# A new written-out order for a fused linear-attention and token-mixing kernel, with constant matmuls ahead of the work, some wider tiles and joint reciprocals

## The chip, the cores and the metric

The kernel runs on one core of one Trainium2 chip. The core has engines that each work through a queue of their own: TensorE (PE, with its weight loads PEld), VectorE (DVE), ScalarE (ACT), GpSimd (POOL) and SyncE (SP), which here only issues DMAs. Times are device microseconds (us) of one execution. The kernel before the change takes 124.98 us, the median of three runs (124.4 to 125.5). The profile is one execution, recorded by the hardware profiler.

## What is computed

Inputs are q, k and v, each of 8 batches x 8 heads x 576 positions x 64, and three weight matrices, all float32. The output is 8 x 576 x 512 in float32. Cut to what matters:

```python
theta = pi/2 * arange(S) / S                      # S = 576
phi(x) = concat([relu(x)*cos(theta), relu(x)*sin(theta)])   # 64 -> 128 features
kv  = phi(k)^T v ;  z = sum_s phi(k)              # per batch and head
x   = (phi(q) kv) / (phi(q) z + 1e-6)             # heads side by side: 576 x 512 per batch
W   = (x w_q)(x w_k)^T / sqrt(64)                 # 576 x 576 per batch
out = relu(W x) w_out
```

The kernel never forms W: it computes `(x w_k)^T x` first, a 64 x 512 matrix, and multiplies `x w_q` with that.

## The kernel before

**Units.** The eight heads of a batch are worked on as two half batches of four heads; half batch H (0 to 15) belongs to batch H // 2. A half batch's q, k or v arrives in two DMAs of 288 KB ("halves" a and b, two heads each). The raw tiles have four buffers per tensor (slot H % 4), nearly all later tiles two. PSUM is one tile of 8 banks, and each PE step names the bank, or the first of two, that it writes.

**Steps.** The whole program is a list of words, `ORDER`. A word is a step's letters, the index, `:bank` for PE, and `@A`, `@V` or `@G` for a step that runs on ACT, DVE or POOL. The loop at L436 to L449 walks through the words and issues each step's instructions, so that every engine's queue holds its steps in the order of the words; waits between engines follow from the tiles that the steps read and write. There is no planner at run time: an engine whose next step has to wait stands still, whatever lies behind it.

- LK, LQ, LV (L131): loads on SP. LW (L417): the weights; w_out is one DMA of 1,024 KB. ST (L414): a store of one 128 x 512 result tile, on SP as well, so a store that waits for its tile holds up every load behind it.
- TK, TV, TQ, TW, T2, TI, TZ: sine tables, identity, zeroed padding.
- RK, RQ (L203): relu of k and q into bf16. CV (L210): v into bf16. VS (L213, DVE): v times cosine and sine.
- KV (L229, PE): k'v of a half batch, 36 small matmuls of 64 x 64 weights with 130 columns, and KE (L250): its copy out of PSUM. QT (L241, PE): q transposed, 18 transposes of 64 x 128. QM (L254, DVE): transposed q times cosine and sine.
- N (L263, PE): numerator and denominator of a quarter batch g (two per half batch, H = g // 2), 20 matmuls. EP (L276): denominator plus epsilon. X (L283, DVE): a reciprocal (L288) and the division (L289).
- XT or XR (PE): x transposed, by 10 whole or 20 half tiles; XE: its copy.
- WK, WQ, KX, MX (PE) with their copies KW, QW, XK, XA, XB, ME: the token mixing of a batch; MX and ME come four to a batch. WO (L400, PE): four matmuls of 128 x 512 for one of 36 output tiles; OE (L408): its copy; CW: casts of the weights.

WO tiles of two batches need the ME steps of those batches, so the first WO can't come before about the first four half batches are through; from then on PE alternates between WO and the steps of later half batches.

Of the kernel before, what the change touches and what calls it, by code (L numbers as in the profile page):

```python
# [29 lines left out]
LK4b RQ5@G LV7b X6 KW0@V EP7@A LQ6b LQ7a KV2:4 LV7a KE2@A N5:4 N4:6 LQ6a LK7b LK7a LV6a CV5@G CW0@A  # L30
X7 RK5@G WQ0:0 KX0:1 LV6b LK6a XT3:2 EP5@A EP4@A X5 XK0@A XA0@A QW0@A X4 LK6b LW2 QT5:4 XT2:6 VS5
MX0:0 QM5 XE3@A CV4@G RQ4@V XE2@A LV9a KV5:2 MX1:6 WQ1:4 ME0@A QT4:0 VS4 KE5@A ME1@A RK4@G N11:2
RQ7@G WK1:5 QM4 QW1@A EP11@A KW1@A N10:6 KX1:5 XB0@A EP10@A LQ9b KV4:0 LV9b XK1@A XA1@A X10 KE4@A
X11 CV7@G LV8b XB1@A N8:0 EP8@A N9:6 LQ9a LK9b X8 MX6:4 XT5:2 RQ6@G RK7@G LK9a EP9@V ME6@A MX2:4 X9
XE5@A VS7 QT7:0 XT4:6 ME2@A MX7:4 KV7:2 LQ8a XE4@A LV8a QM7 WK2:6 MX3:0 LK8a ME7@A QT6:4 KE7@A LQ8b
MX5:2 LK8b CV6@G KW2@A RK6@G CW5@G LQ10b KX2:6 ME3@A LQ11b WQ2:7 VS6 ME5@A QM6 N15:2 KV6:0 LV11
CW2@G MX4:4 XK2@A CV9@G RQ9@G EP15@V XB2@G QW2@A CW3@A X15 CW4@V KE6@A RK9@G LQ10a LV13b N14:6 N12:0
N13:2 ME4@A EP14@V LQ11a RQ8@G EP12@A WO6:4 LK11a X14 WO0:5 LK11b EP13@A XT7:6 X12 WO2:0 OE6:0@A
LV10b LK10b X13 XT6:2 RK8@G XA2@A WO8:1 XE7@A MX8:6 OE0:1@A QT9:4 VS9 XE6@V OE2:2@A CV11@G LV10a
OE8:3@A LK10a LK13b QM9 LK12a WK3:0 ME8@A CV8@A KV9:2 KW3@V KE9@V MX11:6 WQ3:1 KX3:0 ME11@A N18:2  # L40
MX9:6 MX10:4 QW3@A XK3@A EP18@A VS8 LV13a WO1:0 ME10@A X18 ME9@A QT8:4 OE1:4@A N19:2 EP19@A QM8
KV8:6 KE8@V WO10:0 N17:6 LV12b EP17@A RQ10@A X19 XB3@G N16:4 WO12:1 WO9:2 EP16@V LV12a RQ11@G LQ13b
OE10:5@A LK13a X17 OE9:6@A WO3:0 X16 XR8:4 XR9:2 RK11@G OE3:7@A XE8@A XA3@A QT10:6 WO4:0 CV10@G
QT11:4 VS11 OE4:8@A XE9@V LQ13a QM10 KV11:2 RK10@G ST2 OE12:9@A WK4:0 KE11@A MX15:2 CV13@G QM11
LV15b LQ12a MX12:6 ST1 LQ12b WQ4:1 ME15@A LV14b ME12@A N23:4 VS10 N22:2 RK13@G KW4@A MX13:6 EP22@V
LK12b ME13@A WO7:0 KV10:6 EP23@V X22 KX4:2 LV14a ST10 QW4@A KE10@A OE7:10@A X23 XK4@A RQ13@G N21:6
N20:4 LQ15b EP21@A VS13 MX14:2 XA4@A RQ12@G WO11:0 CV12@A WO5:1 ME14@A LQ15a OE11:2@A ST7 LQ14b X21
EP20@V KV13:6 KE13@A QT13:2 X20 LQ14a XR10:4 MX16:6 WO14:0 ME16@A OE5:4@A XB4@G VS12 XT11:6 WO16:1
QM13 XE11@V RK12@G XE10@A N27:2 MX18:4 LV15a OE16:11@A ME18@A EP27@A QT12:6 WO15:1 ST11 RQ15@G
OE14:5@A KV12:4 ST3 WQ5:0 QM12 X27 KE12@A CV14@G MX17:4 N26:6 LK15a EP26@V CV15@G MX19:2 QW5@A  # L50
ME17@A X26 ST5 WK5:0 ME19@A N24:4 OE15:10@V N25:2 XR13:6 LK15b KW5@A EP24@A ST15 KX5:0 RK15@G EP25@V
WO19:1 XE13@A WO21:6 XK5@A X25 X24 RQ14@A WO17:0 OE21:4@A OE19:7@A QT15:4 ST16 QT14:6 XR12:2 VS15
XE12@A LK14a WO13:1 QM15 KV15:4 XA5@A ST14 VS14 WK6:2 KE15@A LK14b OE13:5@A WO20:3 N31:4 QM14
OE17:11@A OE20:10@V EP31@V XB5@A ST20 RK14@V MX22:0 KW6@A MX21:6 ME22@A KX6:2 WQ6:3 ME21@A X31
KV14:0 N30:6 ST9 QW6@A XK6@A XA6@G MX20:4 ME20@A MX23:2 ST21 KE14@V WO18:0 XB6@G N29:4 ME23@A ST12
ST0 ST13 EP30@V X30 OE18:10@V EP29@A MX26:2 ST4 N28:6 EP28@A WO23:1 WO24:0 ME26@A MX25:2 ST6 X29
OE23:2@A OE24:4@A XR15:4 X28 XR14:6 WO26:0 XE15@V ST24 OE26:5@A WO25:1 XE14@V ME25@A OE25:8@V WK7:0
ST23 MX27:2 MX24:6 ME24@V ST26 KW7@A WQ7:1 KX7:0 ST18 XK7@A ST25 QW7@A ME27@V XB7@G WO22:6 WO28:7
XA7@A MX31:0 OE22:2@V OE28:10@A MX28:2 WO27:6 ST8 ME31@A MX30:0 ST19 ST28 OE27:3@A MX29:4 ME30@V
# [6 lines left out]
def kernel(  # L66
# [162 lines left out]
    def KV(H, ps, eng):  # L229
        place["KV", H] = ps  # L230
        kv_v = kv_view(ps)
        for c in range(C):
            for pr, r in ((0, 0), (1, 1), (1, 0), (0, 1)):
                a = slice(H2 * r, H2 * r + H2)
                o = slice(H2 * pr, H2 * pr + H2)
                nc.tensor.matmul(  # L236
                    kv_v[o, r, :], rk_b[H % NPREP][a, pr, c, :],
                    v2_b[H % NV2][a, pr, c, :, 0:D + 1],
                    start=(c == 0), stop=(c == C - 1))

    def QT(H, ps, eng):  # L241
        place["QT", H] = ps
        qt_v = qt_view(ps)
        for c in range(C):
            for r in range(2):
                a = slice(H2 * r, H2 * r + H2)
                nc.tensor.transpose(qt_v[:, r, c * H2:(c + 1) * H2],  # L247
                                    rq_b[H % NPREP][a, c, :, :], ident[a, a])
# [4 lines left out]

    def QM(H, ps, eng):  # L254
        V.tensor_mul(  # L255
            qm_b[H % NQM][:, :, :, 0:C, :].rearrange("p s r c d -> p s r (c d)"),
            qt_view(place["QT", H]).unsqueeze(1).to_broadcast([P, 2, 2, S]),
            qtab.rearrange("p s c d -> p s (c d)").unsqueeze(2).to_broadcast([P, 2, 2, S]))
# [4 lines left out]
    def N(g, ps, eng):  # L263
        H, r = divmod(g, 2)
        place["N", g] = ps
        nv = num(ps)
        for u in range(SC):
            for s in range(2):
                for pr in range(2):
                    a = slice(H2 * pr, H2 * pr + H2)  # L270
                    nc.tensor.matmul(  # L271
                        nv[:, pr, u, :], qm_b[H % NQM][a, s, r, 2 * u:2 * u + 2, :],
                        kv_b[H % 2][a, r, s, 0:D + 1],
                        start=(u == 0 and s == 0), stop=(u == SC - 1 and s == 1))

    def EP(g, ps, eng):  # L276
        den = num(place["N", g])[:, :, :, D:D + 1]
        if eng is A:
            A.activation(rec_b[g % 8], den, AF.Identity, bias=eps_t)  # L279
        else:  # L280
            V.tensor_scalar(rec_b[g % 8], den, EPS, None, op0=ALU.add)

    def X(g, ps, eng):  # L283
# [4 lines left out]
        V.reciprocal(rec, rec)  # L288
        V.tensor_tensor(  # L289
            x_b[b % NX][:, :, 4 * h:4 * h + 4, :].rearrange(  # L290
                "p u (w r) d -> p r w u d", r=2)[:, r],
            nv[:, :, :, 0:D], rec.to_broadcast([P, 2, SC, D]), op=ALU.mult)
# [187 lines left out]
```

## Time and profile before

| | |
|---|---|
| median of three runs | 124.98 us |
| span of the profiled execution, first to last instruction | 122.35 us |
| DMA traffic of the kernel | 39.07 MB |
| last matmul ends | 118.64 us into the span |

The span is 2.63 us shorter than the median; the time of a run also has what lies outside the first and last instruction. In the pages of the profile each line is a group of instructions with its busy time, and the chain of waits is followed back from the last instruction. The clock row is the TensorE clock that the profiler recorded. Matmuls are pipelined, so that the mean duration of one matmul is longer than the time by which it moves the queue; the latter is read from the chain, which gives whole runs of matmuls by their length.

### The profile page before, as it was taken

How to read it: one execution, taken by the hardware profiler on the slowest of the kernel's cores; microseconds unless marked ns; L12 is line 12 of the kernel's file. 1: busy time of each engine (PE TensorE's matmuls, PEld its weight loads, DVE VectorE, ACT ScalarE, POOL GpSimd, SP SyncE). 2: the span in 40 equal slices, each digit the busy share in tenths (PEclk: the TensorE clock that was granted, in tenths of full speed). 3: DMA queues.
4: the chain of work that ended last, by engine and by line, in shares of the span. 5: the costliest groups of instructions: out<-in, count | busy, mean ns of one | idle time of the engine just before them, and what ended most of it. 6: DMA issues, size and time to landing. Idle time of an engine off the chain costs nothing.

```text
span 122.3 us, 5248 instructions
## 1 busy us (share of the span) xinstructions
PE 97.3 (80%) x2250; PEld 65.4 (53%) x2266; DVE 92.0 (75%) x136; ACT 80.8 (66%) x151; POOL 55.2 (45%) x63
## 2 busy tenths in 40 slices
PE   0015878859987796989997959899999999999970
PEld 0013766758776574656572636556765665563420
DVE  0226999896998996997989695996899998764420
ACT  7245858612888886587935837889787986557260
POOL 7764030747369999777492386548120020010000
PEclk9999999999999999999999999999999999999997
DMA  3999999999999999999999996399249069596975
GB/s 115 311 379 404 397 389 388 385 404 384 393 391 384 399 401 397 391 390 396 390 393 392 408 392 259 117 331 296 105 152 303 1 250 358 188 351 259 359 267 211
DMA packets 20614, 39.39 MB, mean 322 GB/s; under 512 B 3184, under 2 KB 3184, under 8 KB 20592
## 3 DMA queue, kind: packets, MB, share of 16 engines
q1 hardware_dynamic: 20592, 39.07, 87.1%
q8 instruction: 17, 0.28, 0.9%
q14 instruction: 5, 0.04, 0.1%
HBM read 29.62 MB, written 9.44 MB: 319 GB/s over the span
## 4 chain that ended last, share of the span: by engine, by line
PE 61%; DMA 18%; issue 7%; DVE 5%; ACT 5%; SPq 1%; DVEq 0%; ACTq 0%
PE ps L405 24%; PE ps L271 8%; PE ps L236 6%; DMA qraw<-in_q_dram 5%; PE ps L335 5%; DMA vraw<-in_v_dram 5%; DMA kraw<-in_k_dram 4%; PE ps L362 4%; PE ps L247 3%; PE ps L348 3%; DMA out_dram<-o 3%; PE ps L302 3%; PE ps L385 3%; DVE x L289 3%; PE ps L315 2%
## 5 line engine op out<-in xcount | busy, mean ns | idle before, releaser
L405 PE MATMUL ps<-wow,mix 128*128 128x512 bf16 x128 | 33.5, 381 | 2.0 <-issue 1.0
L215 DVE TENSOR_TENSOR v<-vb,vtab 128x2304 bf16<-128x2304 bf16 (+1 forms) x17 | 23.4, 1374 | 6.2 <-POOL vb L197 6.2
L289 DVE TENSOR_TENSOR x<-ps,rec 128x640 bf16<-128x640 f32 x32 | 26.4, 825 | 1.9
L255 DVE TENSOR_TENSOR qm<-ps,qtab 128x2304 bf16<-128x2304 bf16 x16 | 21.5, 1351 | 3.1 <-PE ps L247 3.1
L195 ACT COPY o<-ps 128x512 f32<-128x512 f32 x29 | 16.5, 587 | 9.2 <-PE ps L405 7.7
L191 POOL TENSOR_SCALAR rk<-kraw 128x1152 bf16<-128x1152 f32 (+1 forms) x13 | 17.2, 1320 | 8.6 <-ACT mix L396 2.8
L236 PE MATMUL ps<-v,rk 64*64 64x130 bf16 x576 | 13.4, 243 | 9.5 <-ACT rk L189 8.9
L405 PEld LDWEIGHTS <-mix 128*128 128x128 bf16 x144 | 12.5, 98 | 15.6 <-issue 2.9
L271 PE MATMUL ps<-kvs,qm 64*128 64x65 bf16 x640 | 16.2, 203 | 4.7 <-ACT kvs L195 1.7
L396 ACT ACTIVATE mix<-ps 128x576 bf16<-128x576 f32 x28 | 17.7, 654 | 3.2 <-PE ps L385 2.6
L197 POOL TENSOR_SCALAR vb<-vraw 128x1152 bf16<-128x1152 f32 (+1 forms) x14 | 15.1, 1082 | 9.9 <-DMA vraw<-in_v_dram 6.7
L191 POOL TENSOR_SCALAR rq<-qraw 128x1152 bf16<-128x1152 f32 (+1 forms) x11 | 14.2, 1296 | 11.4 <-DMA qraw<-in_q_dram 5.1
L271 PEld LDWEIGHTS <-qm 64*128 64x128 bf16 x640 | 13.8, 102 | 8.4 <-issue 5.3
L236 PEld LDWEIGHTS <-rk 64*64 64x64 bf16 x576 | 10.7, 120 | 12.4 <-ACT rk L189 9.1
L195 ACT COPY xT<-ps 128x1280 bf16<-128x1280 bf16 (+1 forms) x11 | 12.9, 1178 | 2.2 <-PE ps L302 1.1
L197 POOL TENSOR_SCALAR kx<-kx 64x256 bf16<-64x256 bf16 x6 | 2.8, 463 | 24.0 <-ACT kx L195 11.4
L247 PE MATMUL ps<-ident,rq 64*128 64x64 bf16 x288 | 8.1, 203 | 1.6 <-issue 0.8
L195 ACT CAST kvs<-ps 128x260 bf16<-128x260 f32 x12 | 4.6, 380 | 6.6 <-PE ps L236 6.5
L335 PE MATMUL ps<-wkw,xT 128*128 128x64 bf16 x160 | 6.9, 200 | 2.5 <-issue 2.5
L247 PEld LDWEIGHTS <-rq 64*128 64x128 bf16 x288 | 6.3, 102 | 4.6 <-issue 3.0
L385 PE MATMUL ps<-wq,kx 64*128 64x288 bf16 x64 | 8.2, 287 | 0.4 <-ACT xT L195 0.3
L279 ACT ACTIVATE rec<-ps,eps 128x10 f32<-128x10 f32 x18 | 4.9, 270 | 5.2 <-PE ps L271 4.5
(48 smaller groups left out, 109.4 us busy)
## 6 DMA issues: line engine op xcount, KB each, us to landing
vraw<-in_v_dram SPq DMA_DIRECT2D x32, 288.0 KB, 6.0
qraw<-in_q_dram SPq DMA_DIRECT2D x32, 288.0 KB, 6.0
kraw<-in_k_dram SPq DMA_DIRECT2D x32, 288.0 KB, 5.9
out_dram<-o SPq DMA_DIRECT2D x36, 256.0 KB, 3.1
wof<-in_moe_w_out_dram SPq DMA_DIRECT2D x1, 1024.0 KB, 7.7
wkf<-in_moe_w_k_dram SPq DMA_DIRECT2D x1, 128.0 KB, 6.1
wqf<-in_moe_w_q_dram SPq DMA_DIRECT2D x1, 128.0 KB, 5.4
```

The source lines that it names most:

```text
L191: eng.tensor_scalar(dst, s, FMAX, 0.0, op0=ALU.min, op1=ALU.max)
L195: A.copy(dst, s)
L197: G.tensor_scalar(dst, s, 1.0, 1.0, op0=ALU.mult, op1=ALU.mult)
L215: V.tensor_mul(v2_b[H % NV2][:, part, :, :, 0:D], vb_b[H % NPREP][:, part].unsqueeze(3).to_broadcast([P, n, C, 2, D]), vtab.unsqueeze(1).t ...
L236: nc.tensor.matmul(kv_v[o, r, :], rk_b[H % NPREP][a, pr, c, :], v2_b[H % NV2][a, pr, c, :, 0:D + 1], start=(c == 0), stop=(c == C - 1))
L247: nc.tensor.transpose(qt_v[:, r, c * H2:(c + 1) * H2], rq_b[H % NPREP][a, c, :, :], ident[a, a])
L255: V.tensor_mul(qm_b[H % NQM][:, :, :, 0:C, :].rearrange("p s r c d -> p s r (c d)"), qt_view(place["QT", H]).unsqueeze(1).to_broadcast([P, ...
L271: nc.tensor.matmul(nv[:, pr, u, :], qm_b[H % NQM][a, s, r, 2 * u:2 * u + 2, :], kv_b[H % 2][a, r, s, 0:D + 1], start=(u == 0 and s == 0), ...
L289: V.tensor_tensor(x_b[b % NX][:, :, 4 * h:4 * h + 4, :].rearrange("p u (w r) d -> p r w u d", r=2)[:, r], nv[:, :, :, 0:D], rec.to_broadca ...
L335: nc.tensor.matmul(o[:, u * DH:(u + 1) * DH], xT_b[b % NXT][:, m, 2 * u:2 * u + 2, :], wkw[:, m, :], start=(m == 0), stop=(m == NDM - 1))
L396: A.activation(dst, s, AF.Relu, scale=scale_moe)
L405: nc.tensor.matmul(o, mix_b[bp % 2][:, m, rt * P:(rt + 1) * P], wow[:, m, :], start=(m == 0), stop=(m == NDM - 1))
```

## The change

The list of words is replaced as a whole: all loads, steps and stores stand in a new order, some steps are on another engine, and some that took a whole half batch are now two halves (or the other way round). Beside the order:

- `WU34`: 34 matmuls of a constant 128 x 128 tile with 192 columns of it are the first work of PE. Nothing reads their result. `TB` on DVE writes the constant.
- `QT` of half batches 3, 4, 6 and 11 is 9 transposes of 128 x 128 in place of 18 of 64 x 128; `QM` of these is then two DVE instructions of 1,152 elements in place of one of 2,304.
- `KV` of half batch 4 is 18 matmuls with 260 columns in place of 36 with 130; half of what it computes is not used, and `KE` copies 520 elements per partition in place of 260.
- The reciprocal is a step of its own: `RC` for one quarter batch (12 times) or `RJ` for both of a half batch in one instruction (10 times).
- w_out is loaded by four DMAs of 256 KB (`LW2` to `LW5`).
- `VG` is new and is called nowhere.

How many steps of a kind each engine has, where that differs (before, then after; "h" is a half step):

| step | ACT | DVE | POOL |
|---|---|---|---|
| CV | 3, then 3 + 6h | 0, then 1 | 12 + 2h, then 6 + 6h |
| RK | 2 + 1h, then 2 + 6h | 1, then 2h | 12 + 1h, then 4 + 12h |
| RQ | 4 + 1h, then 2 + 7h | 1, then 1h | 10 + 1h, then 7 + 6h |
| EP | 18, then 14 | 14, then 18 | |
| KE | 12, then 15 | 4, then 1 | |
| KW, QW, XK | 22, then 22 | 2, then 2 | |
| XE | 11, then 10 | 5, then 6 | |
| ME | 28, then 27 | 4, then 5 | |
| OE | 29, then 26 | 7, then 10 | |
| XA, XB | 10, then 7 | | 6, then 9 |
| CW | 3, then 2 | 1, then 1 | 2, then 3 |

The diff, cut:

```diff
 ORDER = """
-TK LV0b LQ0a TZ LV0a LK0b TV TQ LK0a T2 LQ0b RK0a@A CV0b@G VS0b LQ1a LV1a TI CV0a@G RQ0a@A LV1b
-RK0b@G LQ1b TW LK1 RQ0b@G VS0a KV0:0 LV3b LV3a LQ3a QT0:2 LK3a LQ3b LK3b LV2a LQ2 LV2b CV1@G KE0@V
-QM0 LW1 RQ1@A VS1 N0:2 EP0@A X0 QT1:0 LK2b N1:4 QM1 EP1@V LK2a RQ3@G LV5b RK1@A LQ5 CV3@A KV1:6 LW0
...
+LV0b LQ0b LV0a LQ1b LQ1a LQ0a LK0a LK0b LV1a LV1b LK1b LK1a LV3b LV3a LV2a LK3a LW1 LK3b LQ3a LQ2a
+LQ3b LQ2b LK2a LW0 LK2b LV2b TI TK TZ TQ TV TB CV0@G T2 WU34:7 RQ1b@A TW RQ1a@V QT1:0 RQ0@A LQ4b
+LQ5b RK0@A VS0 QM1 QT0:2 CV1@A LV5b LQ5a KV0:0 QM0 KE0@A N1:0 RK1b@G RK1a@A VS1 N0:2 KV1:4 EP0@V
+EP1@A KE1@A RJ0 N2:4 CV3@G CW1@G CV2a@A X1 RK3@A RQ3a@A X0 VS2a RQ3b@G EP2@A XR0:2 N3:0 XE0@A VS3
...
+WO14:4 XE11@A OE14:9@A ST14 LQ14b LQ14a LQ15b LV15b LQ15a LV15a ST11 LK15a LK15b ST8 ST0 LV14b LK14a
+LK14b N27:0 RQ12@G MX18:6 EP27@A WO15:5 WO16:4 RC27 X27 MX19:0 RK12a@V ME18@A QT12:6 XE10@A RK12b@G
...
+CV14a@G CV14b@G KE15@A QM15 MX20:0 RK14@G VS14 MX22:4 KW6@A ME20@A ME22@A N31:6 WQ6:3 EP31@V KX6:0
+QW6@A RC31 KV14:4 XK6@A N30:0 KE14@A X31 MX23:6 XA6@G WO18:3 EP30@V OE20:3@A ST20 ST16 ST19 ST10
...
+    QT_WIDE = (3, 4, 6, 11)
+    KV_WIDE = (4,)
...
     def KV(H, ps, eng):
         place["KV", H] = ps
+        if H in KV_WIDE:
+            kv_v = kv_wide(ps)
+            for c in range(C):
+                for r in range(2):
+                    a = slice(H2 * r, H2 * r + H2)
+                    nc.tensor.matmul(
+                        kv_v[:, r, :], rk_b[H % NPREP][a, 2 * c * D:2 * (c + 1) * D],
+                        v2_b[H % NV2][a, :, c, :, 0:D + 1],
+                        start=(c == 0), stop=(c == C - 1))
+            return
...
     def QT(H, ps, eng):
         place["QT", H] = ps
+        if H in QT_WIDE:
+            qt_v = qt_wide(ps)
+            for c in range(C):
+                nc.tensor.transpose(qt_v[:, c, :], rq_b[H % NPREP][:, c, :, :], ident)
+            return
...
     def QM(H, ps, eng):
+        if H in QT_WIDE:
+            q_t = qt_wide(place["QT", H]).rearrange("p c (r d) -> p r c d", r=2)
+            for r in range(2):
+                V.tensor_mul(
+                    qm_b[H % NQM][:, :, r, 0:C, :],
+                    q_t[:, r].unsqueeze(1).to_broadcast([P, 2, C, H2]), qtab)
+            return
...
+    def RC(g, ps, eng):
+        V.reciprocal(rec(g), rec(g))
+
+    def RJ(H, ps, eng):
+        V.reciprocal(rec_b[H % 4], rec_b[H % 4])
+
     def X(g, ps, eng):
...
-        V.reciprocal(rec, rec)
...
-            nc.sync.dma_start(wo_f, moe_w_out.rearrange("(c p) n -> p c n", p=P))
+            nc.sync.dma_start(wo_f[:, i - 2, :], moe_w_out[(i - 2) * P:(i - 1) * P, :])
...
+    def TB(i, ps, eng):
+        V.memset(wc, 1.0)
+
+    def WU(i, ps, eng):
+        for _ in range(i):
+            nc.tensor.matmul(bank(ps)[:, 0:WARM_COLS], wc[:, 0:P], wc[:, 0:WARM_COLS],
+                             start=True, stop=True)
```

More of the change, by code (lines that the diff above doesn't have):

```diff
@@ L30 @@
[L30 to L59, printed above, removed]
@@ new lines @@
+KV3:6 RQ2@A CV2b@G LV6b LV5a LV4a LQ4a LV4b LK5b LK5a LK4b LQ6b LK4a LK7a LV7b LQ7b LV6a LV7a LK7b
+LQ7a LW4 LQ6a EP3@V RJ1 RK2@G LK6a LW5 LK6b QT3:2 KE3@A X2 X3 QT2:0 XT1:6 QM3 N6:2 QM2 XE1@A N7:4
+WK0:6 VS2b CW0@A RQ5a@G EP7@V KV2:0 EP6@A KE2@A WQ0:7 RC7 X7 N5:0 RQ5b@G KW0@A RC6 X6 N4:4 KX0:6
+EP5@V QW0@A XK0@A XA0@G RC5 QT5:2 EP4@A CV5@A CV4a@G X5 RC4 X4 XR3:0 RQ4@G CV4b@G XR2:4 XB0@G VS5b
+XE2@V VS5a MX1:6 XE3@A QM5 MX0:0 ME1@A VS4 ME0@A WK1:4 RK4b@G QT4:6 RK4a@G RK5a@A CV7@G WQ1:5 RQ7@G
+LQ11a LW2 LW3 LV8b LQ9b LQ9a LV9b LV9a LQ8a LK9a RK5b@A LK9b LV8a LK8b LK8a LQ8b KV5:2 KW1@A KX1:4
@@ new lines @@
+MX15:2 MX13:6 QT10:4 ME13@A QM10 ME15@A WQ4:1 WK4:0 MX12:2 RK10a@A N23:6 KW4@A QW4@A EP23@A N22:4
+WO7:0 VS10 ME12@A EP22@V KV10:2 RJ11 RK13@G KX4:1 CV13@A KE10@A OE7:9@A ST7 LQ12b LK12b LK12a XK4@A
+X22 MX14:2 X23 RQ13@G CV12@G ME14@A XB4@G VS13 N20:4 N21:6 WO11:1 EP21@V WO5:0 OE11:10@A EP20@V
+XA4@A RJ10 OE5:11@A ST5 ST12 X20 X21 KV13:2 MX16:4 QT13:0 KE13@V QM13 XR11:6 ME16@A VS12 XR10:2
+WO14:4 XE11@A OE14:9@A ST14 LQ14b LQ14a LQ15b LV15b LQ15a LV15a ST11 LK15a LK15b ST8 ST0 LV14b LK14a
+LK14b N27:0 RQ12@G MX18:6 EP27@A WO15:5 WO16:4 RC27 X27 MX19:0 RK12a@V ME18@A QT12:6 XE10@A RK12b@G
@@ L201, with rk_of @@
     flat = "p r c d -> p r (c d)"
+    def rk_of(H):
+        if H in KV_WIDE:
+            return rk_b[H % NPREP].rearrange("p (c r d) -> p r c d", r=2, d=D)
+        return rk_b[H % NPREP].rearrange("p (r c d) -> p r c d", r=2, d=D)
     def RK(H, ps, eng, part):
-        relu(eng, rk_b[H % NPREP].rearrange(flat)[:, part], raw["k"][H % NRAW][:, part])
+        relu(eng, rk_of(H)[:, part], raw["k"][H % NRAW].rearrange("p r (c d) -> p r c d", d=D)[:, part])
     def RQ(H, ps, eng, part):
@@ L218, in VS, with VG @@
             vtab.unsqueeze(1).to_broadcast([P, n, C, 2, D]))
+    def VG(H, ps, eng, part):
+        n = part.stop - part.start
+        dst = v2_b[H % NV2]
+        s = raw["v"][H % NRAW].rearrange("p r (c d) -> p r c d", d=D)
+        if H in VG_SPLIT:
+            for t in range(2):
+                G.tensor_mul(dst[:, part, :, t, 0:D], s[:, part],
+                             vtab[:, :, t].unsqueeze(1).to_broadcast([P, n, C, D]))
+        else:
+            G.tensor_mul(dst[:, part, :, :, 0:D],
+                         s[:, part].unsqueeze(3).to_broadcast([P, n, C, 2, D]),
+                         vtab.unsqueeze(1).to_broadcast([P, n, C, 2, D]))
     def pair(i):
@@ L430, in CW @@
             cast(eng, wow[:, m, :], wo_f[:, m, :])
-    steps = {f.__name__: f for f in (KV, QT, KE, QM, N, EP, X, XT, XR, XE, WK, KW, WQ, QW, KX, XK, XA, XB,
+    wc = pool.tile([P, 256], BF16, name="warm")
+    def TB(i, ps, eng):
[4 more added lines that the diff above has]
+                             start=True, stop=True)
+    steps = {f.__name__: f for f in (RC, RJ, TB, WU, KV, QT, KE, QM, N, EP, X, XT, XR, XE, WK, KW, WQ, QW, KX, XK, XA, XB,
                                      MX, ME, WO, OE, ST, LW, CW, TK, TV, TI, TQ, TW, T2, TZ)}
-    halves = {f.__name__: f for f in (RK, RQ, CV, VS)}
+    halves = {f.__name__: f for f in (RK, RQ, CV, VS, VG)}
     for word in ORDER.split():
@@ L440 @@
         word = word.rstrip("ab")
-        kind = word[:2] if word[:2] in steps or word[0] in "LRCVT" else word[0]
+        kind = word[:2] if word[:2] in steps or word[:2] in halves or word[0] in "LT" else word[0]
         i, ps = int(word[len(kind):] or 0), int(ps or 0)
```

59 lines of the change are left out of this document (45 added, 14 removed).

## The prediction

> **What bounds the kernel now.** I read the page first: busy times, then the slices of the span.
>
> ```profile
> PE 97.3 (80%) x2250; PEld 65.4 (53%) x2266; DVE 92.0 (75%) x136; ACT 80.8 (66%) x151; POOL 55.2 (45%) x63
> ...
> PEclk9999999999999999999999999999999999999997
> DMA  3999999999999999999999996399249069596975
> ```
>
> No engine is busy throughout, and DMA is full only until about 73 us. The shares mix stages, so I cut the span where the work changes (the view of stages; columns: length, busy time and count of PE, PEld, DVE, ACT, POOL, granted clock, DMA share, GB/s).
>
> ```profile
> 0.00:8.59 8.59, 0.00 (x0) 0.00 (x0) 1.52 (x2) 3.67 (x8) 5.96 (x20) 1.00 0.78 259
> 8.59:32.00 23.41, 18.32 (x464) 15.38 (x464) 19.72 (x29) 13.19 (x22) 9.85 (x9) 1.00 1.06 393
> 32.00:75.83 43.83, 37.27 (x978) 25.52 (x983) 37.86 (x55) 32.70 (x63) 31.31 (x25) 1.00 1.04 389
> 75.83:118.64 42.81, 41.70 (x811) 24.50 (x820) 32.90 (x52) 30.66 (x60) 8.10 (x9) 1.00 0.67 234
> 30.75:73.20 42.45, 35.96 (x935) 25.04 (x938) 38.16 (x52) 31.23 (x60) 29.97 (x25) 1.00 1.05 394
> ```
>
> The last 43 us belong to PE: 1.1 us idle. In the middle neither PE (6.6 us idle) nor DVE (4.3 idle of 42.45) is free; they feed each other. The first stage holds a surprise, which the chain of waits in order of time shows (start, us, what):
>
> ```profile
> 30.93 1.18 PE ps L302 x10
> 32.12 0.37 PE ps L247 x18
> 32.48 0.68 PE ps L302 x10
> ```
>
> The same ten transposes take 1.18 us before 32.0 us and 0.68 after: until then PE runs at half rate, although the clock column says 1.00 (nothing is recorded ahead of the first change). Slots of 3.41 us around that point and around the recorded drop at the end tell what switches it:
>
> ```profile
> 25.18:28.59 3.41, 2.89 (x85) 2.66 (x85) 2.59 (x7) 0.95 (x3) 2.30 (x2) 1.00 1.06 399
> 28.59:32.00 3.41, 3.41 (x35) 2.47 (x29) 3.20 (x5) 1.24 (x4) 2.30 (x2) 1.00 1.04 388
> 69.55:72.96 3.41, 1.91 (x75) 1.57 (x74) 3.41 (x3) 1.72 (x4) 2.12 (x2) 1.00 1.04 400
> 117.34:120.75 3.41, 1.30 (x7) 0.39 (x4) 0.36 (x1) 1.17 (x2) 0.00 (x0) 1.00 0.96 359
> 120.75:124.16 3.41, 0.00 (x0) 0.00 (x0) 0.00 (x0) 0.00 (x0) 0.00 (x0) 0.50 0.08 28
> ```
>
> A slot 85% busy did not lift the rate, one 100% busy did; at full rate 56% kept it, and after 38% it was gone at 120.75.
>
> **The change part by part.**
>
> *PE.* Full-rate prices, by runs in the chain:
>
> ```profile
> 81.34 0.29 PE ps L315 x20
> 82.72 0.56 PE ps L302 x10
> 84.56 0.12 PE ps L385 x2
> 85.92 0.65 PE ps L236 x35
> 86.57 0.61 PE ps L348 x8
> 87.41 0.31 PE ps L271 x20
> 87.84 0.69 PE ps L335 x20
> 108.44 0.55 PE ps L362 x10
> 112.49 6.16 PE ps L405 x28
> ```
>
> So a WO costs 4 x 0.22 = 0.88, N 0.31, KV 0.65, WK 0.69, WQ 0.61, KX 0.55, MX 0.12, XR 0.29, XT 0.56, QT 0.37 (32.12 above). A wide QT is nine of L302's transposes, 9 x 0.056 = 0.50 (bounds 0.37, no change, and 0.61 at 0.068): +0.13 x 4 = 0.5. The wide KV is 18 matmuls of 260 columns; by L385's 0.06 for 288 columns in half rows it is 0.98, by L348's 0.076 1.24; I take 0.98 (L385 has the same half-row tiles): +0.33. One XR in place of an XT: -0.27. In sum +0.6 us.
>
> *The constants.* 34 x 192 columns at 0.056 to 0.118 us per 128 (the L302 rows, full and half rate) is 2.9 to 6.0 us. They can start when DVE has written them, about 0.9 us, and end by 6.9 at the latest. The first real PE step needs q of half batch 1, at about 8.5 (below), so their own cost is nothing. But 1.6 us or more of idling follow, and from 8.5 to 12 PE has two QT and a piece of KV, 1 to 1.9 us. Such slots lie around 38%, the slot that lost the clock. I take it that the first stage runs at half rate as before. [...]
>
> *DVE*, and in the last row ACT. Mean times:
>
> ```profile
> L289 DVE TENSOR_TENSOR x<-ps,rec 128x640 bf16<-128x640 f32 x32 | 26.4, 825 | 1.9
> L215 DVE TENSOR_TENSOR v<-vb,vtab 128x2304 bf16<-128x2304 bf16 x15 | 21.8, 1456 | 0.2 <-POOL vb L197 0.2
> L255 DVE TENSOR_TENSOR qm<-ps,qtab 128x2304 bf16<-128x2304 bf16 x16 | 21.5, 1351 | 3.1 <-PE ps L247 3.1
> L288 DVE RECIPROCAL rec<-rec 128x10 f32<-128x10 f32 x32 | 6.7, 211 | 1.3 <-ACT rec L279 0.9
> L199 DVE COPY o<-ps 128x512 f32<-128x512 f32 x7 | 4.8, 688 | 4.3 <-PE ps L405 4.0 <-PE ps L271 0.3
> L398 DVE TENSOR_SCALAR mix<-ps 128x576 bf16<-128x576 f32 x4 | 2.8, 752 | 2.1 <-PE ps L385 2.1
> L199 DVE COPY xT<-ps 128x1280 bf16<-128x1280 bf16 x3 | 2.4, 821 | 1.0 <-PE ps L315 1.0
> L215 DVE TENSOR_TENSOR v<-vb,vtab 128x1152 bf16<-128x1152 bf16 x2 | 1.5, 760 | 6.0 <-POOL vb L197 6.0
> L191 DVE TENSOR_SCALAR rk<-kraw 128x1152 bf16<-128x1152 f32 x1 | 0.7, 745 | 0.0
> ...
> L189 ACT ACTIVATE rq<-qraw 128x1152 bf16<-128x1152 f32 x4 | 4.7, 1164 | 1.9 <-DMA qraw<-in_q_dram 1.9
> ```
>
> A joint reciprocal replaces two of 0.211 by one of 20 elements. Its price lies between 0.21 and 0.42; I take 0.22, because ten elements more are little beside the 640 that cost 0.825: -0.2 x 10 = -2.0. Wide QM: two of 0.76 for one of 1.35, +0.17 x 4 = 0.7. Steps moved here: OE +3 (2.1), EP +4 (0.65), ME +1 (0.75), XE +1 (0.8), CV +1 (0.75, as RK). Moved away: three KE (-1.3), half an RQ (-0.6). DVE gains nothing: about +1.8 in all. Between X4 and VS10, the stretch of 30.75 to 73.20 above, the order puts 12 X, 8 VS and 8 QM, as before, but four XE for two, and CV, ME and OE: 42.2 us at mean times, against 40.1 counted the same way for before. That is +2.1.
>
> *ACT* takes 6.5 half batches of CV, RK and RQ from POOL and DVE, 7.5 us at the last row's 1.16, and gives away OE, EP, XE, XA and XB: about +2 us on 80.8. POOL has some 6 us less. Both lie beside PE and DVE, which are fuller; that cover is gone where a KE on ACT, for which PE waits, stands behind a half step (0.6).
>
> *The start.* Loads land in the order of SP's queue. The first V of half batch 1 was ninth:
>
> ```profile
> 7.18 0.82 POOL L191 TENSOR_SCALAR rk<-kraw 128x576 bf16<-128x576 f32 x1 [0.50 <-DMA kraw<-in_k_dram]
> ...
> 10.89 1.15 POOL L197 TENSOR_SCALAR vb<-vraw 128x1152 bf16<-128x1152 f32 x1 [1.61 <-DMA vraw<-in_v_dram]
> ...
> 16.11 0.82 DVE L289 TENSOR_TENSOR x<-ps,rec 128x640 bf16<-128x640 f32 x1
> ...
> 29.93 0.82 DVE L289 TENSOR_TENSOR x<-ps,rec 128x640 bf16<-128x640 f32 x1
> ```
>
> Fourth at 7.18, ninth at 10.89: 0.74 each. After the change q of half batch 1 is fourth and fifth (7.9), so QT1 starts at 8.5; k of half batch 0 is seventh and eighth (10.1, before fourth and fifth). RK0 ends at 11.35, KV0 (at half rate 1.3) at 12.6, and KE0 stands behind CV1 on ACT until 13.1. N1 and N0 end at 14.5, one joint reciprocal, X1 and X0 end at 16.6, where before they ended at 16.9. Further on: q3 lands twentieth (19.4 with the small weight ahead), QT3 ends at 21.2, XT1 at 23.6, N7 at 24.9, KV2 27.4, WQ0 28.5, N4 29.8, X4 31.4, against 30.75. From 22.4 on PE has no gap, so a full slot lifts the rate between 25.8 and 29.2, not at 32.0. I take X4 at 31.0: +0.25.
>
> *w_out in four pieces* moves no byte more; its landing is waited for by nobody before WO0.
>
> *Sum.* X4 +0.25. DVE to VS10 +2.1, of which I let half fall into the 4.3 us of idle time: +1.0. KV10, which starts the last stage, began 2.6 us after VS10, held by PE's queue, so part of that delay is absorbed; PE itself has +0.8 by then (all wide steps) and an earlier full rate: KV10 +0.8. After it the same steps remain with 1.1 us idle in 42.81, and the last WO, copy and store are as before: +0.1. In sum +0.9: 122.35 becomes 123.25, and with the 2.63 between span and median 125.9. Within 1% (123.7 to 126.2) a measurement of this kernel can't tell it from no change.
>
> **The rivals.**
>
> 1. *The constants hold the full rate.* Then the first stage goes by loads: k2 and v2 land last of the first four half batches, at 22.9; RK2 on POOL ends at 24.95, KV2 at 25.65, N4 at 26.65, X4 at 28.0 in place of 31.0. DVE's own 20.7 us of steps from 7.9 allow that. -3.0: 122.9. For it: 34 dense matmuls fill a slot. Against: the 38% slot. [...]
>
> 2. *The order feeds PE better in the middle.* If half of its 6.6 us of idling goes, -3.3: 122.6. For it: halves free raw buffers earlier and POOL is emptier. Against: DVE's stretch is fuller by 2.1.
>
> 3. *Slower: the loads of half batch 14 come behind ST14.* SP may issue ST14 only when WO14 is copied (0.6); eleven half loads and three more stores stand between it and the end of k14, 4.29 MB with ST14 itself. From WO14 to KV14 PE has 7 WO, 5 N, 6 MX, 3 QT, 2 each of KV, WK, WQ, KX and XR: 15.1 us at the prices above, and 16.5 by what the last stage took (42.81 us for steps that these prices count as 39.2).
>
> ```profile
> 79.79:83.20 3.41, 3.25 (x93) 2.28 (x93) 3.38 (x4) 2.98 (x7) 1.76 (x3) 1.00 1.00 345
> ```
>
> At 393 GB/s, loads alone, the bytes take 10.9 us; at the 345 of this slot, in which loads and stores mix at a full DMA share, 12.4. With the copy, 2 us from issue to landing and RK14 on POOL (1.4) that is 15 to 16.5. It decides from 16.5 on: at 250 GB/s (17.2 us) it is 21.2, and KV14 and all behind it come 4.7 late. Middle of that: +3, 129.
>
> **How the numbers follow.** The forecast has 0.43, with its own range 123.5 to 128; rival 1 0.2, rival 2 0.12, rival 3 0.25. Faster by over 1%: most of rivals 1 and 2 and a seventh of the forecast, 0.30. Slower by over 1%: rival 3 and two fifths of the forecast, 0.43. The rest, 0.27, is within 1%. The range takes in both fast rivals, with DVE's idle time wholly used at its low end (121.8), and the middle of rival 3 with a little more (130).
>
> **What would show it.** The ten transposes of the first XT1 at 1.1 us and a PE first reaching full rate between 25.8 and 29.2 us bear out the clock step; 0.56 would show rival 1. X4 near 31 and VS10 1 us later than 73.2 bear out the DVE sum; a PE idle time of 3 us in the middle is rival 2. A wait of PE for rk or v at KV14 is rival 3. I am wrong altogether if one wait in the new order, such as a KE behind half steps on ACT, stops PE for several us at a place that I have not walked.

## The result, and the profile after

The changed kernel takes 128.88 us, the median of four runs (127.49 to 130.62); the kernel before, beside it, took 124.69 (123.61 to 125.5). The ratio is 1.0314, with a 95% interval of 1.0213 to 1.0414: about 3% slower. Ratios here and below are taken from undisturbed runs alone, so that they need not equal the quotient of the medians. The profiled execution of the changed kernel is the slowest of its four, with a span of 128.7 us (the others 125.5 to 127.4), so I read places and causes from it, and sizes from the ratios and from the other runs.

Its page, busy times and slices:

```profile
PE 106.4 (83%) x2242; PEld 73.5 (57%) x2256; DVE 94.9 (74%) x140; ACT 84.5 (66%) x156; POOL 54.4 (42%) x70
...
PEclk9995555599689779999999999999999779999999
DMA  4999999779999979999499959985999903959894
```

The row to look at is DMA. Before, it was full until 73 us without a break. Now it has holes from the eighth slice on, and 7s and 5s throughout. The clock row shows what the row of before couldn't: a rate that is lost and comes back several times.

The stages, cut at the same places of the work as before (first step of PE on data, end of X4, end of VS10, start of KV10 to the last matmul):

```profile
0.00:8.67 8.67, 5.23 (x35) 4.77 (x36) 1.17 (x3) 4.57 (x8) 4.55 (x18) 1.00 0.77 270
8.67:31.86 23.19, 16.93 (x473) 14.13 (x473) 18.96 (x29) 14.35 (x25) 7.97 (x10) 0.63 0.96 329
31.86:77.58 45.72, 40.50 (x913) 28.63 (x919) 39.83 (x58) 33.47 (x66) 25.61 (x27) 0.93 0.92 323
77.80:125.10 47.30, 43.56 (x823) 25.99 (x830) 34.83 (x53) 31.34 (x58) 16.31 (x16) 0.96 0.82 292
```

X4 ends at 31.86 (30.75 before), VS10 at 77.58 (73.20), KV10 starts at 77.80 (75.83), the last matmul ends at 125.1 (118.64). The third stage has DMA at 0.92 and 323 GB/s, where the like stretch of before had 1.05 and 394. In the fourth, loads still come in (POOL has 16.31 us of work there, 8.10 before), and the stage takes 47.30 us in place of 42.81.

The costliest groups name who waited, by the idle time ahead of them:

```profile
L198 POOL TENSOR_SCALAR rk<-kraw 128x576 bf16<-128x576 f32 (+1 forms) x16 | 19.4, 1214 | 18.3 <-DMA kraw<-in_k_dram 15.4
L198 POOL TENSOR_SCALAR rq<-qraw 128x1152 bf16<-128x1152 f32 (+1 forms) x13 | 13.5, 1041 | 15.4 <-DMA qraw<-in_q_dram 15.2
L204 POOL TENSOR_SCALAR vb<-vraw 128x1152 bf16<-128x1152 f32 (+1 forms) x12 | 11.4, 953 | 13.8 <-DMA vraw<-in_v_dram 11.8
```

POOL waited 42 us for loads. That alone costs nothing; the chain below shows where PE waited for POOL. And SP, whose queue issues the loads (the view of waits, for SP):

```profile
SPq L480 <- ACT o L202: 14.1, 8, 6.0
SPq L141 <- DMA vraw<-in_v_dram: 12.0, 13, 3.7
SPq L480 <- ACT kx L202: 6.7, 2, 4.3
```

L480 is the store. Of the first row only 2.7 us lie ahead of the last load, which is issued at 96.8 us; its longest wait, 6.0 us, comes later and holds up stores alone. Ahead of the last load a store whose tile is not written yet stands at the head of SP's queue for up to 4.3 us (the third row), and the loads behind it stand too. The chain of waits shows what that did to the end of the profiled execution (start, us, what):

```profile
85.10 0.59 ACT o L202
...
85.71 0.33 SPq L480
...
91.83 6.95 DMA kraw<-in_k_dram
...
100.00 1.16 POOL rk L198
...
```

ACT writes result tile 14, ST14 goes out, six loads and a store are issued one by one, then the two loads of k of half batch 15, of which the second is issued at 91.8 and lands at 98.8. POOL ends a step of its own (1.12 us more), then does the relu, and only then KV15 can start: PE waits for k behind ST14. PE's own order of time shows a second wait beside it (in brackets the idle time ahead and what ended it):

```profile
100.10 0.30 PE L450 MATMUL ps<-wq,kx 64*128 64x288 bf16 x2 [1.54 <-ACT o L202]
101.20 1.03 PE L278 MATMUL ps<-v,rk 64*64 64x130 bf16 x36 [0.80 <-POOL rk L198]
```

The step ahead of KV15, MX21, needs the bank that OE17 copies out. OE17 waited 1.42 us for its result buffer, which ST8 had to empty first; ST8 stands behind the loads of k of 15 and landed at 99.4. So SP's queue held PE in two ways at once, and mending one of them would have left the other.

### The profile page after: what moved, and what is told of

Read it like the earlier page. It is cut to its first block, busy times and chain, and to the rows that moved or that the text cites. A ratio compares the mean times of both kernels' runs of the same rounds, so it can differ in the third digit from the quotient of the medians.

```text
span 128.7 us, 5249 instructions
## 1 busy us (share of the span) xinstructions
PE 106.4 (83%) x2242; PEld 73.5 (57%) x2256; DVE 94.9 (74%) x140; ACT 84.5 (66%) x156; POOL 54.4 (42%) x70
## 4 chain that ended last, share of the span: by engine, by line
PE 33%; DMA 11%; DVE 8%; POOL 6%; SPq 4%; ACT 4%; issue 2%; POOLq 0%; DVEq 0%
PE ps L470 14%; DMA kraw<-in_k_dram 11%; POOL rk L198 4%; SPq L141 4%; PE ps L329 3%; PE ps L278 3%; PE ps L450 3%; DVE x L354 2%; DVE qm L313 2%; PE ps L400 2%; PE ps L427 2%; PE ps L367 2%; PE ps L413 2%; ACT mix L461 1%; PE ps L294 1%
## 5 line engine op out<-in xcount | busy, mean ns | idle before, releaser
L198 POOL TENSOR_SCALAR rk<-kraw 128x576 bf16<-128x576 f32 (+1 forms) x16 | 19.4, 1214 | 18.3 <-DMA kraw<-in_k_dram 15.4
L202 ACT COPY o<-ps 128x512 f32<-128x512 f32 x26 | 15.3, 587 | 9.1 <-PE ps L470 6.6
L313 DVE TENSOR_TENSOR qm<-ps,qtab 128x2304 bf16<-128x2304 bf16 x12 | 16.1, 1352 | 1.9 <-PE ps L294 1.9
L204 POOL TENSOR_SCALAR vb<-vraw 128x1152 bf16<-128x1152 f32 (+1 forms) x12 | 11.4, 953 | 13.8 <-DMA vraw<-in_v_dram 11.8
L278 PE MATMUL ps<-v,rk 64*64 64x130 bf16 x540 | 13.1, 244 | 3.8 <-ACT rk L196 2.0
L202 ACT CAST kvs<-ps 128x260 bf16<-128x260 f32 (+1 forms) x15 | 5.9, 395 | 9.6 <-PE ps L278 8.8
L204 POOL TENSOR_SCALAR kx<-kx 64x256 bf16<-64x256 bf16 x9 | 4.8, 531 | 13.8 <-DVE kx L206 10.2
L294 PE MATMUL ps<-ident,rq 64*128 64x64 bf16 x216 | 5.9, 202 | 4.9 <-DVE rq L198 2.3
L196 ACT ACTIVATE rq<-qraw 128x576 bf16<-128x576 f32 (+1 forms) x9 | 7.0, 784 | 3.4 <-DMA qraw<-in_q_dram 3.4
L196 ACT ACTIVATE rk<-kraw 128x576 bf16<-128x576 f32 (+1 forms) x8 | 6.3, 800 | 3.8 <-DMA kraw<-in_k_dram 3.7
L294 PEld LDWEIGHTS <-rq 64*128 64x128 bf16 x216 | 4.7, 102 | 7.1 <-ACT rq L196 3.6
```

The costliest lines, as they stand in the source:

```text
L196: A.activation(dst, s, AF.Relu)
L198: eng.tensor_scalar(dst, s, FMAX, 0.0, op0=ALU.min, op1=ALU.max)
L202: A.copy(dst, s)
L204: G.tensor_scalar(dst, s, 1.0, 1.0, op0=ALU.mult, op1=ALU.mult)
L278: nc.tensor.matmul(kv_v[o, r, :], rk_of(H)[a, pr, c, :], v2_b[H % NV2][a, pr, c, :, 0:D + 1], start=(c == 0), stop=(c == C - 1))
L313: V.tensor_mul(qm_b[H % NQM][:, :, :, 0:C, :].rearrange("p s r c d -> p s r (c d)"), qt_view(place["QT", H]).unsqueeze(1).to_broadcast([P, ...
```

## The experiments

The runs of the kernel before beside these had medians of 124.36 to 124.87 us.

**Constants away.**

```diff
-LQ3b LQ2b LK2a LW0 LK2b LV2b TI TK TZ TQ TV TB CV0@G T2 WU34:7 RQ1b@A TW
+LQ3b LQ2b LK2a LW0 LK2b LV2b TI TK TZ TQ TV CV0@G T2 RQ1b@A TW
```

> The changed kernel without its 34 constant matmuls. Theory A (the clock that they lift at 5.86 us is lost again at 9.27, before work in any number runs): no change, 128.0 to 129.5, and full rate first at about 26 us all the same. Rival (the constants help, by work done at full rate from 8.6 to 9.3): slower by 0.5 us or more. Rival (they cost, by moving the phase of later drops): faster by 0.5 us or more.

130.03 us (127.12 to 133.43), ratio 1.0359 [1.0189, 1.0529]. Within what can be measured that is the changed kernel, but the interval is 3.4% wide, so an effect of the 34 products of 1 or 2% either way is not excluded. The trace bears out the expectation: the full rate comes first at 26.7 us, against 26.3 with the constants.

**SP's queue, three ways.** Some loads and stores change their place in the list; the engines' own steps stay. The first four lines are the front and the middle, the last two the tail. The front alone moves LV6b and LQ11a and leaves LV13b and ST1 where they were; all three together also move LV14a and ST7, which the lines leave out.

```diff
-KV3:6 RQ2@A CV2b@G LV6b LV5a LV4a ... LQ7b LV6a
+KV3:6 RQ2@A CV2b@G LV5a LV4a ... LQ7b LV6b LV6a
-LQ11a LW2 LW3 ... LV13b LV11b ... ST1 LK11a LQ11b ... LV10a LK10a LV13a
+LW2 LW3 ... LV11b ... LK11a LQ11a LQ11b ... LV10a ST1 LK10a LV13b LV13a
...
-ST5 ST12 ... ST14 LQ14b LQ14a LQ15b LV15b LQ15a LV15a ST11 LK15a LK15b ST8 ST0 LV14b LK14a LK14b
+LQ14b LQ14a LQ15b LQ15a ST5 ST12 LV15b LV15a LK15a LK15b LV14b LK14a LK14b ST14 ST11 ST8 ST0
```

The tail alone:

> Only the last part of SP's queue mended: the loads of half batches 14 and 15 no longer stand behind ST14, ST11, ST8 and ST0. Theory B: the wait of 2.3 us ahead of KV15 and the half clock that follows it (1.7) go, 125 to 126. Rival (k15 was late because all loads were late since 20 us): 127.5 or more, with the wait still there or moved to another half batch.

The front alone; with LQ11a behind its reader, half of q of half batch 11 is not the input there, here and in the run with all three:

> Only the front of SP's queue mended: LV6b and LQ11a, which held SP from 21.2 to 25.5 and from 42.2 to 44.9 us, stand later. Theory B: the loads of half batches 4 to 9 land up to 4 us earlier, 1 to 2 us faster, 126.5 to 128. Rival (PE and DVE had enough to do there): no change, 128.5 to 129.5.

All three:

> The changed kernel with the order of SP's queue alone mended: six loads and stores that wait for a buffer or a result are moved behind the loads that they held up. Theory B (SP's queue holds loads back, and these are late at KV9, KV11 and KV15): 123.5 to 125.5, PE's wait ahead of KV15 gone, DMA share ahead of 60 us near 1.0. Rival C (the fuller DVE and the wide tiles set the time): 127.5 or more, although the loads come earlier.

Tail: 130.28 (128.91 to 132.56), 1.0494 [1.0386, 1.0602]. Front: 128.16 (126.97 to 130.27), 1.0329 [1.0218, 1.044]. All: 132.7 (131.99 to 137.45), 1.0735 [1.0648, 1.0823]. None is faster than the changed kernel beyond what can be measured, and all three together are much slower. The trace of the last says why. Its chain of waits, and then its waits by who waited for whom (total, times, longest):

```profile
62.21 6.50 DMA out_dram<-o
...
68.81 0.59 ACT o L202
```

```profile
PE ps L470 <- ACT o L202: 4.1, 1, 4.1
```

ST1 had been moved behind eight loads. Its result tile was not free again when the copy of WO12, which uses the same of the 12 result buffers, came up on ACT; so ACT waited, and PE behind it 4.1 us. Moving a store back needs a free buffer for what comes after it. The edit also made a stop of its own: LQ11a behind its reader can't be issued before that has read the buffer, and SP issued nothing from 50.8 to 58.2 us. With the tail alone the wait moved in the same way: PE stood 2.17 us for ACT up to 92.7 and 1.74 up to 100.1. So none of the three decided on the loads; the next two do.

**Loads first, with buffers enough.** 24 result buffers for 12, the eight stores that stood ahead of the last load go behind it, and LV6b, LQ11a, LV13b and LV14a stand later, ahead of their readers.

```diff
-    NRAW, NPREP, NV2, NQM, NX, NXT, NOUT = (4, 2, 2, 2, 2, 2, 12)
+    NRAW, NPREP, NV2, NQM, NX, NXT, NOUT = (4, 2, 2, 2, 2, 2, 24)
-... LV11a ... ST1 LK11a ... LQ12a ... ST7 LQ12b ... LK12a ... ST5 ST12 ... ST14 LQ14b ... LV15a ST11 LK15a LK15b ST8 ST0 LV14b LK14a LK14b
+... LV11a ... LK11a ... LQ12a ... LQ12b ... LK12a ... LQ14b ... LV15a LK15a LK15b LV14a LV14b LK14a LK14b ST1 ST7 ST5 ST12 ST14 ST11 ST8 ST0
```

> The changed kernel with 24 result buffers in place of 12 and no store ahead of the last load in SP's queue; LV6b, LQ11a, LV13b and LV14a, which waited there for a raw buffer, stand behind the loads that they held up. Work, engines and order of all other steps are those of the changed kernel. Theory B (loads that SP holds back, together with copies that wait for a result buffer, cost the 4 us): 124 to 126, k15 there before PE needs it. Rival C (fuller DVE and wide tiles, PE's own waits): 127.5 or more.

125.98 us (125.08 to 128.12), 1.0216 [1.0126, 1.0306]. By the medians some 3 us of the 4.2 are back; by the ratios, whose intervals overlap, 1%. The stretch from 32 to 76 us, first in the kernel before:

```profile
32.00:76.00 44.00, 37.44 (x990) 25.70 (x998) 38.03 (x55) 32.71 (x63) 31.31 (x25) 1.00 1.03 388
```

in the changed one:

```profile
32.00:76.00 44.00, 38.89 (x870) 27.49 (x877) 38.11 (x55) 31.75 (x62) 25.09 (x27) 0.92 0.92 323
```

and in this one:

```profile
32.00:76.00 44.00, 38.79 (x963) 27.19 (x963) 41.31 (x60) 34.51 (x69) 27.46 (x29) 1.00 1.04 387
```

DMA is full again, the rate holds, and DVE gets 60 instructions done where the changed kernel got 55. VS10 ends at 74.2.

**The same buffers, SP's order left alone.** This separates the two halves of the edit above.

> The changed kernel with 24 result buffers in place of 12 and nothing else: SP's queue stands as in the changed kernel, ST14 and the stores and loads in front of it too. Theory A: what delays the loads is that stores and buffer waits stand ahead of them in SP's queue; more result buffers don't change that, so the time stays near the changed kernel's, 128 to 129. Rival B: ScalarE's copies waiting for result buffers were the cost, and loads that stand behind stores merely follow: then this one comes near the loads-first version, 126.0.

128.97 us (127.27 to 131.18), 1.033 [1.0245, 1.0414]: the changed kernel's time. The interval still overlaps that of loads first; the medians differ by 3.0 us. The middle has its holes again:

```profile
32.00:76.00 44.00, 37.30 (x864) 25.50 (x857) 38.55 (x55) 30.90 (x61) 23.18 (x25) 0.96 0.88 316
```

The chain of waits passes ST14 again, but it now ends at k of 14 and KV14:

```profile
85.84 0.59 ACT o L203
...
86.45 0.33 SPq L481
...
89.72 4.67 DMA qraw<-in_q_dram
...
95.16 6.36 DMA kraw<-in_k_dram
...
101.69 2.31 POOL rk L199
...
```

```profile
104.04 0.72 PE L279 MATMUL ps<-v,rk 64*64 64x130 bf16 x36 [0.36 <-POOL rk L199]
```

PE stands for 0.36 us there and not at all ahead of KV15, and still the time is that of the changed kernel. So the wait at the end is not what most of the time went for. The profiled executions, cut at three steps, say where it went:

| us into the span | before | changed | buffers only | loads first |
|---|---|---|---|---|
| VS10 ends | 73.20 | 77.58 | 78.06 | 74.22 |
| KV10 starts | 75.83 | 77.80 | 78.24 | 74.54 |
| last matmul ends | 118.64 | 125.10 | 123.34 | 119.33 |

Buffers only and loads first differ by SP's order alone. Of the 4.0 us between their last matmuls, 3.8 are there when VS10 ends, in the middle, where the one moves 316 GB/s and the other 387. So it is the order of SP's queue, and the buffers only make another order possible. The changed kernel's own profile adds the waits ahead of KV15.

**The kernel before, treated the same way** (24 buffers, all its stores behind LK14b):

> The kernel before with 24 result buffers and no store ahead of the last load. Theory (the last 43 us belong to PE, which had 1.1 us idle there; the loads of before were early enough): no change, 124 to 125.5. Rival (before, too, loses to SP's queue): 123 or less.

124.47 us (123.65 to 125.51), 1.0114 [1.0009, 1.0218], by the medians no change. There the stores, though they stand among the loads too, had cost next to nothing.

**What the clock is worth.** The kernel before, with 56 constant products at the start and 8 of 128 columns behind each of the first 21 steps of PE.

```diff
+TB WU56:7
-... KV0:0 LV3b LV3a LQ3a QT0:2 LK3a ...
+... KV0:0 WF8 LV3b LV3a LQ3a QT0:2 WF8 LK3a ...
```

> The kernel before with 56 constant matmuls ahead of its work and 8 small ones of 128 columns behind each of its first 21 PE steps, so that no slot of 3.41 us from 4 to 30 us is idle. Theory (the rate is held by the busy share of a slot; full rate early brings X4 forward by about 3 us, DVE then limits): full rate from 8 us on at the latest, 121.5 to 123.5. Rival (DVE and the loads set the first 30 us, and the constants delay real steps): 124.5 or more in spite of the full rate. Rival (constant matmuls between do not hold the rate): the clock falls to 0.5 within 15 us.

131.97 us (130.77 to 133.9), 1.068 [1.0576, 1.0783]. The rate was full from 6.4 to 33.7 us, as meant, and the kernel slower, since those who wait for a step now wait for the products behind it (waits of DVE; L445 is the constant products):

```profile
DVE rec L282 <- PE ps L445: 4.0, 2, 2.7
```

How much an early full rate is worth by itself stays open.

**Narrow tiles.** The changed kernel, and then the loads-first version, without the wide QT, QM and KV:

```diff
-    QT_WIDE = (3, 4, 6, 11)
-    KV_WIDE = (4,)
+    QT_WIDE = ()
+    KV_WIDE = ()
```

> The changed kernel with every QT, QM, KV and KE in the narrow form of before. By the sum: PE -0.8 us and DVE -0.7 us, part of it hidden: 0.3 to 0.8 us faster, 128.0 to 128.8. Rival (wide tiles cost what the change lost): 126 or less.

> The loads-first version of the new order (24 result buffers, stores behind the last load) without the wide tiles: the four QT and the one KV in their old form. Theory A: the wide tiles cost PE 0.13 each for QT and 0.33 for KV and DVE 0.17 for each wide QM, 1.5 us of engine time of which about half lies on the path, and the 2.7 us by which narrow tiles made the changed kernel slower came from SP's queue alone. Then this one is about 0.8 us below the loads-first version: 125.2. Rival B: the order needs the wide tiles (a wide QT has one producer and one write less to wait for), and narrow tiles cost here what they cost there: 128.5.

131.62 (131.16 to 132.93), 1.0705 [1.0615, 1.0794], and 127.78 (126.8 to 130.24), 1.0273 [1.0198, 1.0349]. Narrow tiles are slower in the first case beyond doubt, and in the second by 1.8 us of median, with intervals that overlap. Both narrow versions lost the full rate in two slots (42 to 49 us), which the loads-first version with wide tiles did not. In both, the slot that lost it holds a pause of PE, of 1.44 and 1.07 us, in which it waited for nothing that the profile shows (such pauses are taken up in the last section). That the pause lost the rate is not shown.

**Single reciprocals** in the loads-first version, each joint one split in two at its place:

```diff
-RJ0 N2:4
+RC0 RC1 N2:4
```

> The loads-first version with each joint reciprocal split into two of one half batch each, back to back at the same place. Theory A: a joint one takes 0.28 us and two single ones 0.42 to 0.44, so ten places cost DVE 1.5 us more, about half of it on the path: 126.7. Rival B: what the joint reciprocal costs is that X of the first half batch waits for both copies of the denominators; the split, which keeps the place, does not undo the wait, so only A's price can show, and if DVE has slack where these stand the time stays at 126.0.

125.23 us (124.02 to 127.98), 1.012 [1.0061, 1.018], the fastest of the new order. The split costs nothing; a gain of 0.75 can't be told from none, as the intervals overlap.

**The order alone**: loads first, with narrow tiles, single reciprocals and no constants.

> The loads-first version without wide tiles, without joint reciprocals and without the constant products: of the whole change only the order of the work on the engines is left, freed of SP's queue. Theory A: the order alone costs what is left of the sum, DVE about 2 us more between X4 and VS10 by the steps moved to it, half of it on the path, so 125 to 126, about 1 above the kernel before. Rival B: the tiles, the reciprocals and the constants are the rest, and the order alone is as fast as before: 124.4. If it is above 127, splitting and narrowing cost more than the order, against both.

129.0 us (127.26 to 130.82), 1.033 [1.0244, 1.0415], above both expectations. Against the run before it, whose interval lies wholly below, only the tiles and the constants are missing; leaving out the constants made no difference in the first run that could be measured, though one of this size, 2%, would just have been within its interval. So this points to the tiles without proving it. The two traces point to a way: between 39 us and the end of X16 PE stands 4.5 us in pauses of that kind here and 0.9 in the run before it, and X16 ends 4.4 us later (70.2 and 65.9). That is one execution of each. No version of the new order beats the kernel before.

## Why the prediction was right, and where not

The measured 128.88 lies in the range (121.8 to 130.0), slower was the likeliest of the three signs, and the time is rival 3's (129), not the forecast's own (125.9). That it came out so near 129 is in part luck: the middle of 0 and 4.7 is 2.4, which gives 128.3 and not 129, and most of the time was not lost where rival 3 looked for it.

**The start was as walked up to X0**, which ends at 16.5 (16.6 predicted). Then it falls behind: QT3 ends at 22.1, not 21.2.

```profile
21.00 1.12 PE L288 MATMUL ps<-ident,rq 128*128 128x128 bf16 x9 [0.65 <-ACT xT L202]
22.69 1.25 PE L367 MATMUL ps<-ident,x 128*128 128x128 bf16 x10
```

Ten transposes of the first XT1 at 1.25 us, half rate, and the record has the rate up at 26.3 us, inside the 25.8 to 29.2 of the prediction. The constants filled one slot (PE is busy throughout from 2.45 to 5.86 us, where the record has the rate up), and in the next one PE was busy for 29%, 0.99 of 3.41 us; at its end, 9.27 us, the record has the rate down again, for 17.07 us. Rival 1 is out. X4 at 31.86 is 0.9 later than the 31.0 I took, and 0.5 later than the 31.4 of the walk. SP had stood from 21.2 to 25.5 us, with LV6b, but that is not what made X4 late: it comes at 31.75 in the loads-first version, where SP doesn't stand there.

**DVE.** Its steps between X4 and VS10 take 39.83 us against 38.16: +1.7 where +2.1 was worked out. A joint reciprocal is dearer than taken:

```profile
L348 DVE RECIPROCAL rec<-rec 128x20 f32<-128x20 f32 x10 | 2.8, 278 | 1.9 <-ACT rec L340 1.1
L345 DVE RECIPROCAL rec<-rec 128x10 f32<-128x10 f32 x12 | 2.5, 211 | 0.4 <-ACT rec L340 0.2
```

0.28 us, not 0.22, so ten save 1.4, not 2.0. Of the term, 1.0 us was to lie on the path. With the loads on time nothing of it does: in the loads-first version the stretch takes 42.47 us (31.75 to 74.22), as before (42.45), with DVE busy for 39.92 of it; its VS10 is 1.0 late because X4 is. So half of the term was too much. In the changed kernel the stretch takes 45.72, 3.3 more than before. That is not the DVE term. What failed is the assumption behind the sum, never stated there, that every load of the middle lands as early as before; I walked SP's queue at the start and at half batch 14 and nowhere between. There SP stopped again and again, as its issues show in order of time (start, us, what):

```profile
41.17 0.98 SPq L141 DMA_DIRECT2D kraw<-in_k_dram  x1
44.92 0.33 SPq L141 DMA_DIRECT2D qraw<-in_q_dram  x1
...
53.85 0.33 SPq L141 DMA_DIRECT2D qraw<-in_q_dram  x1
56.23 1.44 SPq L141 DMA_DIRECT2D vraw<-in_v_dram  x3
62.26 0.35 SPq L480 DMA_DIRECT2D out_dram<-o  x1
...
68.46 1.21 SPq L141 DMA_DIRECT2D kraw<-in_k_dram  x2
74.70 0.33 SPq L141 DMA_DIRECT2D vraw<-in_v_dram  x1
```

Nothing is issued from 42.2 to 44.9 (LQ11a stands for its raw buffer), from 54.2 to 56.2 (LV13b), from 57.7 to 62.3 (ST1, for its tile) and from 69.7 to 74.7 (LV14a). One late load in the chain:

```profile
50.48 6.84 DMA kraw<-in_k_dram
...
57.50 1.38 POOL rk L198
...
63.11 1.32 POOL rq L198
64.43 0.05 issue
64.48 0.46 PE ps L294 x18
```

This is a k that lands at 57.3, POOL busy with what had piled up until 64.4, and PE waiting 1.83 us for QT8.

**The last stage** was to take 0.1 us more, because the same steps remain. They do, but for one XT that is now an XR, and PE is busy for 41.65 us in it in the loads-first version (41.70 before). Yet it takes 44.8 us there, 45.1 with buffers only and 47.3 in the changed kernel, against 42.8. So this step failed too, by 2 us even where no load is late; in the loads-first version 1.76 of them are one pause of PE for nothing that the profile shows. That this version takes 125.98 us, as the forecast has it, is therefore luck as well: its KV10 starts 1.3 us earlier than before, not 0.8 later, and its last stage takes 2.0 more, not 0.1.

**Rival 2** is out as well: PE is idle for 5.2 us between X4 and VS10 (6.5 before), where 3 would have shown it.

**Rival 3** named a mechanism that the profile of the changed kernel shows, a load behind ST14 for which PE waits, but at k of 15, which the order takes ahead of 14. I had walked to KV14 and not to KV15: k of 15 landed 13.1 us after the copy of WO14 had ended (85.7 to 98.8). With buffers only the time is the same and this wait all but gone, so it isn't the cause of most of the loss.

**The rate in the middle** was a term that I left at nothing (56% busy had kept it). The profiled execution of the changed kernel lost it in three more slots. In the other three the mean clock was 0.918 to 0.930, against 0.894 here; if their first stage was like this one, that leaves room for one such slot at most. Two slots that lost it, one that kept it, the third that lost it, and the slot at half rate behind that:

```profile
29.75:33.17 3.42, 1.97 (x70) 1.25 (x64) 3.11 (x5) 3.03 (x5) 2.12 (x3) 1.00 0.96 301
39.99:43.41 3.42, 2.06 (x56) 1.39 (x53) 3.25 (x7) 3.13 (x8) 1.25 (x1) 1.00 1.05 390
60.47:63.89 3.42, 2.15 (x59) 1.48 (x47) 2.49 (x5) 2.33 (x5) 3.34 (x3) 1.00 0.50 178
98.02:101.43 3.41, 1.07 (x37) 0.67 (x40) 2.62 (x2) 1.75 (x4) 3.17 (x4) 1.00 0.97 370
101.43:104.85 3.42, 3.42 (x84) 2.83 (x74) 1.53 (x2) 1.79 (x4) 3.34 (x3) 0.50 0.49 186
```

The stop ahead of KV15 cost twice here: PE idle, and then 3.4 us at half rate, 1.7 us of work lost just where PE bounds. In the loads-first version the rate, once up at 27, stayed up. But late loads do not decide it: it also stayed up from 26.7 us on in the version with the front moved, at 301 GB/s from 32 to 76 us, and the narrow loads-first version lost it at 388.

**The tiles** I priced as a cost: +0.5 and +0.33 on PE, +0.7 on DVE. The price of KV is about right (18 wide products 1.03 us in the chain, against 0.98); a wide QT moved PE's queue by 0.60 to 0.63 us in the loads-first version, from its start to that of the next group, which is the upper bound; in the chain there it took the 0.50 assumed (at 67.79 us). But the time without the wide tiles is not lower: it is clearly higher in the changed kernel, and not to be told apart in the loads-first version. The term had the wrong sign, for a reason I can't show.

**ACT and w_out.** ACT has 84.5 us, +3.7 where +2 was counted. PE's waits for it are short but for the 1.54 us above, and that was a wait for a result buffer. No wait for w_out's pieces appears among PE's.

## What to carry to other kernels

In a queue that issues loads and stores in a written order, walk every entry, not the first and the last: here a store that waited (ST1, 57.7 to 62.3 us) and a load that waited (LV14a, 69.7 to 74.7) were stops for all behind them, and the price showed far away, as an engine that waited for loads (POOL, 42 us in all). Before a store is moved back, count the buffers that the tiles after it need. Don't take the last wait in the chain for the cause of the whole: the wait at the end could all but go (0.36 us of it left) and the time stayed (128.97 us, against 128.88), since the loss lay in the middle. And price a wait of PE not by its length alone, but with the half rate that followed it here (3.4 us at 0.50, behind a slot 31% busy).
